# Power tables in another element order, longer Toeplitz loads and a wider margin in the written order, in an attention and state-space kernel

## Chip, cores and metric

The kernel runs on one core of a Trainium2 chip. The metric is device time in microseconds: the median of the runs. One more execution is recorded by the hardware profiler; all lines of profile and trace below come from that one.

## What is computed

Two branches over the same 2,048 tokens of width 448, mixed by a gate:

```python
g = sigmoid((x * gate_w).sum(-1, keepdims=True))
a = A_ref(x, wq, wk, wv, wo)      # 16 query heads of 28, ONE key and value head, softmax over 2048 keys
b = B_ref(x, A, B, C, log_dt, Dskip)
return g * a + (1 - g) * b

# B_ref: a diagonal state-space layer as a causal convolution, per channel d (448 of them)
K[d, l] = real(sum_n C[d,n] * dB[d,n] * exp(dt[d] * A[d,n] * l))     # n = 256 complex modes, l = 0..2047
y[:, d] = causal_convolution(u[:, d], K[d]) + u[:, d] * Dskip[d]
```

Tensors are bfloat16. Most of the arithmetic is the 16 x 2,048 x 2,048 exponentials of the softmax, the kernel K of 448 channels from 256 modes each, and the convolution of each channel.

## The kernel before

**Attention.** ScalarE takes the exponentials. The work is cut into 1,024 score tiles of 128 keys x 512 queries: 16 groups (`i`, 4 heads and 512 queries each), 16 key tiles, 4 heads. Tiles go in sets of three and two by turns. TensorE writes a set's scores into PSUM (five banks, lines 1103 and 1112), ScalarE takes the exponential of the set in one instruction (L1134) into a ring of 15 buffers, and TensorE multiplies by the values (L1144). For each group there are also a query projection (L759), copies of masked queries by GpSimd's DMA queue, a normalisation (`norm`, L1004 to L1014, with a path through DRAM for the reciprocals) and, every fourth group, the output projection (`outp`, L986) and its gated addition to the result `O` (L995).

**State space.** The 448 channels go in 14 chunks of 32. For each chunk:

1. `masters` (in four blocks of chunks, L796 to L818) squares the complex pole again and again on VectorE, so that powers 1, 2, 4, ... up to 1,024 steps exist.
2. `tables` (L820 to L873) builds on VectorE tables of 32 consecutive powers by doubling: five levels, each with two products (L850, L852), a difference (L854) and a sum (L856). A table row holds 128 values: 64 for the low powers (32 channels, two halves of the modes) and 64 for powers in steps of 32, seeded with the coefficients. The real table and the imaginary table are separate blocks of 33 rows (`BLK`). It also builds `rho` (L859, L863), a further table FM by a reversed product (L867), and negates the imaginary one (L872).
3. `kgen` (L875 to L912) makes K from these tables on TensorE, 128 matmuls of 64 columns per chunk (L889), each for one channel, one half of the modes, and the real or imaginary part. As neighbouring powers lie one row apart, its operands step 128 elements, 256 bytes. VectorE copies the result (L899, L902), and GpSimd's DMA queue writes it to a DRAM scratch tensor KP in nine stores. KP has for each channel a row of 1,088 elements, in two halves.
4. `conv` (L937 to L978), twice per chunk. `tload` (L924 to L935) loads for 4 channels the Toeplitz matrix: partition 2i + h reads the KP row of half h from element i on, 1,024 elements for each of 4 channels. It is two transfers, one per h, of 64 partitions x 4 rows of 2,048 bytes. There are 4 such loads per `conv`, 112 in all; they go to 4 buffers in T and later to up to 3 in the part of U (the input) that is no longer needed. Then 128 matmuls (L949), a gated copy to `cst` (L958), 16 transposing matmuls (L969), and an addition to `O` (L977).

**The order.** Nothing is ordered by hand. Every operation is recorded with an estimated duration, a rank (`pr`, low first), what it reads and writes, and if it needs one of two spare PSUM banks, a lock on one (`lock`, `unlock`). `schedule` (L156 to L276) then plays the whole program through with its own constants and fixes the order of each engine; at run time the engines only follow it and wait on semaphores. The constants that matter here: `SLACK` (L86) is time added to a dependency across engines for operations of rank 2 and up, by engine; `FETCH` (L82) is how long a new block of 256 TensorE instructions is taken to need; L138 and L140 price a DMA by its descriptors. GpSimd's queue carries the KP stores, the masked queries and the normalisation's small transfers; SP's queue carries the Toeplitz loads in order, each waiting for KP of its chunk and for the last reader of its buffer, and the stores of the result behind all of them.

Of the kernel before, what the change touches and what calls it, by code (L numbers as in the profile page):

```python
# [12 lines left out]
P = 128  # L13
# [12 lines left out]
LO = 2 * BLK  # L26
FM = 2 * LO
# [7 lines left out]
TW = 4 * 1024  # L35
# [39 lines left out]
class Prog:  # L75
# [6 lines left out]
    BLOCK, FIRST, FETCH, IDLE, NEED = 256, 172, 5300.0, 3300.0, 0.015  # L82
# [3 lines left out]
    SLACK = {"pe": 500.0, "dve": 300.0}  # L86
# [44 lines left out]
    def dma(self, pairs, desc, slot, rd=(), wr=(), pr=0, eng="sp", slow=False, extra=0):  # L131
# [6 lines left out]
        o = self.op(eng, fn, nd * ns / 16.0 * (1.15 if size < 1500 else 1.8 if nd < 512 else 1.0), rd, wr, pr)  # L138
# [237 lines left out]
class Kernel:  # L376
# [25 lines left out]
    def alloc(self):  # L402
# [26 lines left out]
        self.T = sb("T", NTR * TW + 768, BF)  # L429
# [212 lines left out]
    def xq(self, q):  # L642
        return ((self.xT, 0), (self.T, NTR * TW + 768 - XQ), (self.expT, 9 * 512), (self.expT, 5 * 512))[q]

# [26 lines left out]
    def prep_params(self):  # L671
# [71 lines left out]
        for s in range(2):  # L743
            o = s * LO + 32 * EW
            for comp, val in ((0, 1.0), (1, 0.0)):
                pg.op("dve", lambda e, o=o, comp=comp, val=val: e.memset(self.tab.v(0, P, o + comp * BLK, [[1, 64]]), val), 70,
                      wr=[("lo", s, 0)] + xd, pr=3)
# [72 lines left out]
    def tables(self, c):  # L820
# [6 lines left out]
        mq = lambda lv: self.mq.v(0, P, lv * W2 + 64 * c, [[1, 64]])  # L827
        pr = 50 + 2 * c

        def vo(fn, n, rd, wr, rate=1.92):  # L830
            pg.op("dve", fn, el(n, rate), rd=rd, wr=wr, pr=pr)
        mk = lambda lv: [("mb", lv), ("mb", lv + 6)]
        lk = lambda l: ("lo", s, l)
        vo(lambda e: e.tensor_copy(tab.v(0, P, lo + 31 * EW, [[BLK, 2], [1, 64]]), mbf.v(0, P, mo, [[128, 2], [1, 64]])),
           128, [("mb", 0), lk(0)], [lk(1)])
        vo(lambda e: e.tensor_copy(tab.v(0, P, lo + 31 * EW + 64, [[BLK, 2], [1, 64]]),
                                   self.seedw.v(0, P, c * 64, [[W2, 2], [1, 64]])),
           128, [("w32", b), ("w32b", b), lk(0)], [lk(2)])
        done = [lk(1), lk(2)]
        for lv in range(5):  # L840
# [3 lines left out]
            so, do = lo + (32 - w) * EW, lo + (32 - 2 * w) * EW  # L844
            src = tab.v(0, P, so, [[BLK, 2], [EW, w], [1, EW]])
            dst = tab.v(0, P, do, [[BLK, 2], [EW, w], [1, EW]])
            mr = mbf.v(0, P, m, [[0, 2], [0, w], [1, EW]])
            mi = mbf.v(0, P, m + 128, [[0, 2], [0, w], [1, EW]])
# [3 lines left out]
            vo(lambda e, src=src, mi=mi, w=w, tb=tb, to=to: e.tensor_tensor(  # L852
                tb.v(0, P, to, [[w * EW, 2], [EW, w], [1, EW]]), src, mi, ALU.mult), 2 * n, done + mk(lv), [tk])
            vo(lambda e, do=do, n=n, tb=tb, to=to: e.tensor_tensor(  # L854
                tab.v(0, P, do, [[1, n]]), tab.v(0, P, do, [[1, n]]), tb.v(0, P, to + n, [[1, n]]), ALU.subtract), n, [tk, kr], [kr])
            vo(lambda e, do=do, n=n, tb=tb, to=to: e.tensor_tensor(  # L856
                tab.v(0, P, do + BLK, [[1, n]]), tab.v(0, P, do + BLK, [[1, n]]), tb.v(0, P, to, [[1, n]]), ALU.add), n, [tk, ki], [ki])
            done = done + [kr, ki]
        vo(lambda e: e.tensor_copy(rho.v(0, P, 31 * 64, [[1, 64]]), mq(0)), 64,  # L859
           [("mq", 0)], ["tmp"])  # L860
        for lv in range(5):
            w = 1 << lv
            vo(lambda e, w=w, lv=lv: e.tensor_tensor(rho.v(0, P, (32 - 2 * w) * 64, [[64, w], [1, 64]]),  # L863
                                                     rho.v(0, P, (32 - w) * 64, [[64, w], [1, 64]]),
                                                     self.mq.v(0, P, lv * W2 + 64 * c, [[0, w], [1, 64]]), ALU.mult), w * 64,
               [("mq", lv), "tmp"], ["tmp"])
        vo(lambda e: e.tensor_tensor(tab.v(0, P, FM, [[64, 2], [EW, 32], [1, 64]]),  # L867
                                     tab.v(0, P, lo + 31 * EW, [[BLK, 2], [-EW, 32], [1, 64]]),
                                     rho.v(0, P, 31 * 64, [[0, 2], [-64, 32], [1, 64]]), ALU.mult), 4096,
           done + ["tmp"], ["Fm"])  # L870
        ni = tab.v(0, P, lo + BLK + EW, [[EW, 31], [1, 64]])
# [3 lines left out]
    def kgen(self, c):  # L875
# [6 lines left out]
        for jj in range(8):  # L882
            def mm(e, comp, jj=jj):
                for half in range(2):
                    for g in range(4):
                        o = half * 32 + 8 * g + jj
                        fo = lo + comp * BLK + EW + o
                        mo = FM + comp * 64 + o
                        r = e.matmul(  # L889
                            G.v(32 * g, 32, 64 * jj, [[1, 64]]),  # L890
                            tab.v(0, P, lo + comp * BLK + 64 + o, [[EW, 32]]),
                            tab.v(0, P, fo, [[mo - fo, 2], [EW, 32]]),
# [3 lines left out]
            for comp in range(2):  # L896
                pg.op("pe", lambda e, mm=mm, comp=comp: mm(e, comp), 226, mode="c", ni=16, rd=keys,
                      wr=[X, "kst", "kst2"], pr=1.4, lock=G if jj == 0 and comp == 0 else None)
# [15 lines left out]
    def tbufs(self):  # L914
        n = NC * 8
        home = [(self.T, k * TW, 0) for k in range(NTR)] + [(self.U, k * TW, (k + 1) * 32) for k in range(3)]
# [7 lines left out]
    def tload(self, gi):  # L924
# [6 lines left out]
        lst = []  # L931
        for h in range(2):
            to = bass.AP(tensor=buf.h, offset=h * buf.rs + o, ap=[[2 * buf.rs, 64], [1024, 4], [1, 1024]])
            lst.append((to, dram(self.KP, h * KH + 4 * gi * KW, [[1, 64], [KW, 4], [1, 1024]])))
        self.lastT = pg.dma(lst, (512, 2048), f"T{s}", rd=[("KP", gi // 8), "pad"] + x, wr=w, pr=1, extra=1500).i  # L935

    def conv(self, c):  # L937
# [3 lines left out]
        ps, px = self.grp(), self.grp()  # L941
# [287 lines left out]
```

## Time and profile before

| | us |
|---|---|
| three runs | 541.32, 544.85, 545.44 |
| median | 544.85 |
| the profiled execution | 546.33 |
| its span, first to last instruction | 544.5 |
| ScalarE: exponentials (L1134), 410 instructions | 468.1 busy |
| first exponential starts, last one starts | 30.5, 522.6 |
| TensorE busy, VectorE busy | 451.6, 455.3 |
| kernel matmuls L889: 1,792 | 69.0 busy |
| DMA: bytes moved | 144.55 MB, 265 GB/s in the mean |

The profile page gives for each engine its busy time; several instructions of TensorE overlap, so its busy time is not work at full rate. A group of instructions is written as line, engine, operation, names and shapes, count, then busy time and mean duration of one in ns, and after the second bar the idle time of the engine just before them and what ended it. A wait is written as who waited, for whom, then total us, how often, and the longest. A timeline row gives start and duration in us, and in brackets the idle time before it and what released it. "issue" means that the profile shows nothing that the engine waited for.

### The profile page before, as it was taken

The page shows a single profiled execution, that of the slowest core. Times are in us where ns is not written, and L with a number is a line of the kernel's source. Part 1 is how long each engine was busy: PE and PEld are TensorE (multiplying, and loading weights), DVE is VectorE, ACT ScalarE, POOL GpSimd, SP SyncE. Part 2 cuts the span into 40 slices and gives each one's busy share as a digit, 9 for nine tenths or more (in the row PEclk, how much of TensorE's full clock was granted, in tenths as well). Part 3 has the DMA queues.
Part 4 walks back from the last instruction along what each step waited for, and adds up shares of the span by engine and source line. Part 5 has one row for each costly group of instructions (what it writes and reads, how often), then busy time and mean ns, then how long its engine had stood idle before and what let it go on. Part 6 is the DMA issues. An engine that isn't in the chain of part 4 may idle for free.

```text
span 544.5 us, 20905 instructions
## 1 busy us (share of the span) xinstructions
PE 451.6 (83%) x9463; PEld 226.4 (42%) x9479; DVE 455.3 (84%) x826; ACT 485.9 (89%) x431; POOL 168.1 (31%) x313
## 2 busy tenths in 40 slices
PE   4787679688798989789788898889898898996875
PEld 3522114154353535345344445345454444352443
DVE  2889999999999989889989998989899999912024
ACT  3699899999999989899999999999999998997840
POOL 5017022515142413315215241515225060532100
PEclk9958888999999999899999999999899999998888
DMA  8995691696977697896994998798994999679996
GB/s 254 238 232 151 47 159 30 172 355 206 360 238 247 189 368 244 257 365 216 361 373 136 362 308 305 208 390 273 326 371 144 345 337 353 182 258 321 361 385 194
DMA packets 122401, 144.55 MB, mean 265 GB/s; under 512 B 54196, under 2 KB 60956, under 8 KB 122312
## 3 DMA queue, kind: packets, MB, share of 16 engines
q1 hardware_dynamic: 112312, 133.06, 75.9%
q0 software_dynamic: 9344, 9.59, 7.3%
q8 instruction: 74, 1.21, 0.9%
q10 hardware_dynamic: 656, 0.57, 0.4%
q14 instruction: 15, 0.12, 0.1%
HBM read 128.76 MB, written 5.28 MB: 246 GB/s over the span
## 4 chain that ended last, share of the span: by engine, by line
ACT 30%; PE 27%; DVE 19%; DMA 15%; issue 3%; SPq 0%
ACT expT L1134 30%; DMA T<-KP_scratch 9%; PE psS L1112 6%; DMA U<-KP_scratch 6%; PE psX L889 5%; PE psS L1103 4%; PE psB L1144 4%; PE psS L949 2%; PE psX L949 2%; DVE msq L796 2%; DVE tab L850 2%; DVE mbf L816 2%; DVE seedz L800 1%; PE psS L889 1%; DVE tmp L852 1%
## 5 line engine op out<-in xcount | busy, mean ns | idle before, releaser
L1134 ACT ACTIVATE expT<-psS 128x1536 bf16<-128x1536 f32 (+1 forms) x410 | 468.1, 1317 | 23.1 <-PE psS L1112 11.7
L1112 PE MATMUL psS<-qM,kT 128*32 128x512 bf16 x1660 | 134.3, 400 | 14.0 <-ACT expT L1134 10.6
L1103 PE MATMUL psS<-qT,kT 29*128 29x512 bf16 x609 | 82.9, 400 | 33.4 <-ACT expT L1134 29.6
L1144 PE MATMUL psB<-expT,vaug 128*32 128x512 bf16 x1024 | 104.7, 398 | 0.7 <-issue 0.4
L135 POOL DMA_DIRECT2D KP_scratch<-kstg x126 | 67.8, 546 | 70.7 <-DVE kstg L902 69.2
L850 DVE TENSOR_TENSOR tab<-tab,mbf 128x256 bf16<-128x256 bf16 (+4 forms) x70 | 68.6, 979 | 0.7
L1103 PEld LDWEIGHTS psS<-qT,kT 29*128 29x128 bf16 x609 | 19.9, 91 | 83.3 <-ACT expT L1134 72.9
L135 POOL DMA_DIRECT2D rdenB<-R_scratch x60 | 30.6, 517 | 75.8 <-DMA R_scratch<-denT 56.3
L889 PE MATMUL psX<-tab 128*32 128x64 bf16 x1280 | 49.5, 286 | 0.3 <-issue 0.2
L1112 PEld LDWEIGHTS psS<-qM,kT 128*32 128x32 bf16 x1660 | 30.4, 98 | 45.6 <-ACT expT L1134 34.7
L1144 PEld LDWEIGHTS psB<-expT,vaug 128*32 128x32 bf16 x1024 | 27.4, 96 | 49.9 <-issue 38.2
L135 POOL DMA_DIRECT2D qM<-qT x64 | 32.1, 509 | 43.4 <-DVE gt L638 20.4
L889 PEld LDWEIGHTS psX<-tab 128*32 128x32 bf16 x1280 | 39.4, 135 | 11.3 <-issue 3.9
L949 PE MATMUL psX<-T,U 128*32 128x128 bf16 (+7 forms) x1568 | 34.4, 221 | 9.0 <-DMA T<-KP_scratch 5.9
L135 POOL DMA_DIRECT2D denT<-acc x15 | 11.3, 756 | 97.5 <-DVE acc L1004 97.5
L949 PE MATMUL psS<-T,U 128*32 128x128 bf16 (+7 forms) x1216 | 30.2, 222 | 9.5 <-DMA T<-KP_scratch 6.7
L852 DVE TENSOR_TENSOR tmp<-tab,mbf 128x256 bf16<-128x256 bf16 (+3 forms) x56 | 36.3, 648 | 0.0
L949 PEld LDWEIGHTS psX<-T,U 128*32 128x32 bf16 (+7 forms) x1568 | 26.5, 94 | 20.3 <-DMA T<-KP_scratch 8.1
L867 DVE TENSOR_TENSOR tab<-tab,tmp 128x4096 bf16<-128x4096 bf16 x14 | 32.1, 2290 | 0.4
L852 DVE TENSOR_TENSOR tab<-tab,mbf 128x4096 bf16<-128x4096 bf16 x14 | 31.9, 2278 | 0.0
L949 PEld LDWEIGHTS psS<-T,U 128*32 128x32 bf16 (+7 forms) x1216 | 21.7, 95 | 21.0 <-DMA T<-KP_scratch 6.9
L863 DVE TENSOR_TENSOR tmp<-tmp,mq 128x64 bf16<-128x64 bf16 (+4 forms) x70 | 25.3, 361 | 1.2
(153 smaller groups left out, 553.4 us busy)
## 6 DMA issues: line engine op xcount, KB each, us to landing
T<-KP_scratch SPq DMA_DIRECT2D x174, 512.0 KB, 9.3
U<-KP_scratch SPq DMA_DIRECT2D x50, 512.0 KB, 9.5
rdenB<-R_scratch POOLq DMA_DIRECT2D x60, 64.0 KB
U<-cst SPq DMA_DIRECT2D x1, 3584.0 KB, 19.0
qM<-qT POOLq DMA_DIRECT2D x64, 32.0 KB, 5.2
tab<-in_A_x_dram SPq DMA_DIRECT2D x4, 448.0 KB, 6.2
O<-in_A_x_dram SPq DMA_DIRECT2D x16, 112.0 KB, 2.7
O<-cst SPq DMA_DIRECT2D x1, 1792.0 KB, 27.1
```

The source lines that it names most:

```text
L135: return [e.dma_start(o, i, **kw) for o, i in pairs]
L796: pg.op("dve", lambda e: e.tensor_tensor(m2(msq), z2, z2, ALU.mult), el(2 * n), rd=[kr, ki] + first, wr=["msq"], pr=pr)
L850: vo(lambda e, dst=dst, src=src, mr=mr: e.tensor_tensor(dst, src, mr, ALU.mult), 2 * n, done + mk(lv), [kr, ki])
L852: vo(lambda e, src=src, mi=mi, w=w, tb=tb, to=to: e.tensor_tensor(tb.v(0, P, to, [[w * EW, 2], [EW, w], [1, EW]]), src, mi, ALU.mult), 2 * ...
L863: vo(lambda e, w=w, lv=lv: e.tensor_tensor(rho.v(0, P, (32 - 2 * w) * 64, [[64, w], [1, 64]]), rho.v(0, P, (32 - w) * 64, [[64, w], [1, 64]]),
L867: vo(lambda e: e.tensor_tensor(tab.v(0, P, FM, [[64, 2], [EW, 32], [1, 64]]), tab.v(0, P, lo + 31 * EW, [[BLK, 2], [-EW, 32], [1, 64]]), r ...
L889: r = e.matmul(G.v(32 * g, 32, 64 * jj, [[1, 64]]), tab.v(0, P, lo + comp * BLK + 64 + o, [[EW, 32]]), tab.v(0, P, fo, [[mo - fo, 2], [EW, ...
L949: r = e.matmul(ps.v(32 * j, 32 - 2 * n, 128 * k, [[1, 128]]), self.U.v(0, P, (4 * gi + j) * 32 + 2 * n, [[1, 32 - 2 * n]]), tbuf.v(0, P, t ...
L1103: r = e.matmul(self.psS.v(0, P, 512 * b, [[1, 512]]), kT.v(32 * h, DH + 1, 128 * kt, [[1, 128]]), qT.v(32 * h, DH + 1, 512 * (i % 2), [[1, ...
L1112: r = e.matmul(self.psS.v(32 * j, 32, 512 * b, [[1, 512]]), kT.v(0, P, 128 * kt + 32 * j, [[1, 32]]), self.qM.v(0, P, (i % 2) * XQ + 512 * ...
L1134: pg.op("act", lambda e: e.activation(expT.v(0, P, 512 * es[0], spread(es, n)), self.psS.v(0, P, 512 * bs[0], spread(bs, n)), AF.Exp, scal ...
L1144: r = e.matmul(self.psB.v(32 * h, 32, 0, [[1, 512]]), vaug.v(0, P, 32 * kt, [[1, 32]]), expT.v(0, P, 512 * ring[t], [[1, 512]]), start=(kt ...
```

## The change

- **Tables.** A chunk's tables are laid out with a pair of channels innermost, then real and imaginary part, then the step: four values (8 bytes) per step, 33 steps per pair (`CG` = 132 elements), 64 pairs. Products (L850, L852) cover whole runs; the difference, the sum, the reversed product and the negation touch every other pair of values. The reversed product becomes two instructions. `kgen`'s operands now step 4 elements, 8 bytes; the scheduler's price for eight of its matmuls goes from 226 to 130 ns.
- **Loads.** One transfer of 128 partitions per Toeplitz load, each partition one row of 3 x 1,088 + 1,024 = 4,288 elements, 8,576 bytes, that runs over the unused ends of the rows between. Buffers grow from 4,096 to 4,288 elements, and the three in U come into use 8 loads later.
- **Scheduler.** `SLACK` of VectorE from 300 to 800 ns, `FETCH` from 5,300 to 5,600; a convolution's result and its transposes share one spare PSUM bank; the output projection's rank goes from 2 to 1.2.

```diff
-    BLOCK, FIRST, FETCH, IDLE, NEED = 256, 172, 5300.0, 3300.0, 0.015
+    BLOCK, FIRST, FETCH, IDLE, NEED = 256, 172, 5600.0, 3300.0, 0.015
-    SLACK = {"pe": 500.0, "dve": 300.0}
+    SLACK = {"pe": 500.0, "dve": 800.0}
-TW = 4 * 1024
+TW = 3 * KW + 1024
...
 # tables
-            src = tab.v(0, P, so, [[BLK, 2], [EW, w], [1, EW]])
-            dst = tab.v(0, P, do, [[BLK, 2], [EW, w], [1, EW]])
-            mr = mbf.v(0, P, m, [[0, 2], [0, w], [1, EW]])
+            src = tab.v(0, P, so, [[CG, 64], [2, 2 * w], [1, 2]])
+            dst = tab.v(0, P, do, [[CG, 64], [2, 2 * w], [1, 2]])
+            dc = [tab.v(0, P, do + 2 * k, [[CG, 64], [4, w], [1, 2]]) for k in range(2)]
+            mr = mbf.v(0, P, m, [[2, 64], [0, 2 * w], [1, 2]])
...
-            vo(lambda e, do=do, n=n, tb=tb, to=to: e.tensor_tensor(
-                tab.v(0, P, do, [[1, n]]), tab.v(0, P, do, [[1, n]]), tb.v(0, P, to + n, [[1, n]]), ALU.subtract), n, [tk, kr], [kr])
+            vo(lambda e, dc=dc, tc=tc: e.tensor_tensor(dc[0], dc[0], tc[1], ALU.subtract), n, [tk, kr], [kr])
+            vo(lambda e, dc=dc, tc=tc: e.tensor_tensor(dc[1], dc[1], tc[0], ALU.add), n, [tk, ki], [ki])
...
-        vo(lambda e: e.tensor_tensor(tab.v(0, P, FM, [[64, 2], [EW, 32], [1, 64]]),
-                                     tab.v(0, P, lo + 31 * EW, [[BLK, 2], [-EW, 32], [1, 64]]),
-                                     rho.v(0, P, 31 * 64, [[0, 2], [-64, 32], [1, 64]]), ALU.mult), 4096,
-           done + ["tmp"], ["Fm"])
-        ni = tab.v(0, P, lo + BLK + EW, [[EW, 31], [1, 64]])
+        for k in range(2):
+            vo(lambda e, k=k: e.tensor_tensor(tab.v(0, P, FM + 2 * k, [[EW, 32], [4, 32], [1, 2]]),
+                                              tab.v(0, P, lo + 124 + 2 * k, [[CG, 32], [-4, 32], [1, 2]]),
+                                              rho.v(0, P, 62, [[64, 32], [-2, 32], [1, 2]]), ALU.mult), 2048,
+               done + ["tmp"], ["Fm"])
+        ni = tab.v(0, P, lo + 6, [[CG, 32], [4, 31], [1, 2]])
 # kgen
-                            tab.v(0, P, lo + comp * BLK + 64 + o, [[EW, 32]]),
-                            tab.v(0, P, fo, [[mo - fo, 2], [EW, 32]]),
+                            tab.v(0, P, so, [[4, 32]]),
+                            tab.v(0, P, fo, [[mo - fo, 2], [4, 32]]),
...
-                pg.op("pe", lambda e, mm=mm, comp=comp: mm(e, comp), 226, mode="c", ni=16, rd=keys,
+                pg.op("pe", lambda e, mm=mm, comp=comp: mm(e, comp), 130, mode="c", ni=16, rd=keys,
 # tload
-        for h in range(2):
-            to = bass.AP(tensor=buf.h, offset=h * buf.rs + o, ap=[[2 * buf.rs, 64], [1024, 4], [1, 1024]])
-            lst.append((to, dram(self.KP, h * KH + 4 * gi * KW, [[1, 64], [KW, 4], [1, 1024]])))
-        self.lastT = pg.dma(lst, (512, 2048), f"T{s}", rd=[("KP", gi // 8), "pad"] + x, wr=w, pr=1, extra=1500).i
+        self.lastT = pg.dma([(buf.v(0, P, o, [[1, TW]]), dram(self.KP, 4 * gi * KW, [[1, 64], [KH, 2], [1, TW]]))], (128, 2 * TW), f"T{s}", rd=[("KP", gi // 8), "pad"] + x, wr=w, pr=1, extra=1500).i
 # conv
-        ps, px = self.grp(), self.grp()
+        ps = px = self.grp()
...
-                                     tbuf.v(0, P, to + j * 1024 + 896 - 128 * n, [[1, 128]]),
+                                     tbuf.v(0, P, to + j * KW + 896 - 128 * n, [[1, 128]]),
...
-              el(512), rd=[X, "omq"], wr=[("cst", cs)], pr=2, unlock=ps)
+              el(512), rd=[X, "omq"], wr=[("cst", cs), X], pr=2)
```

## Prediction

> **What bounds the kernel now.** I read the busy shares first, then ScalarE's waits, then what TensorE did just before each of those waits, then the last 30 us, then VectorE's groups by shape.
>
> ```profile
> PE 451.6 (83%) x9463; PEld 226.4 (42%) x9479; DVE 455.3 (84%) x826; ACT 485.9 (89%) x431; POOL 168.1 (31%) x313
> ```
>
> ScalarE is the fullest, and the others are close behind. From its first exponential (30.5 us) to the end of its last (523.2) lie 492.7 us, of which the exponentials fill 468.1. The waits say where the rest is:
>
> ```profile
> ACT expT L1134 <- PE psS L1112: 11.7, 13, 2.4
> ACT expT L1134 <- PE psS L1103: 8.3, 12, 1.5
> ACT expT L1134 <- PE psX L949: 1.3, 1, 1.3
> ACT expT L1134 <- PE psB L1144: 0.9, 1, 0.9
> ```
>
> That is 22.2 us in 27 waits, all for scores that TensorE delivered late. TensorE's timeline ahead of each shows two causes:
>
> ```profile
> 411.81 0.40 PE L949 MATMUL psS<-T,U 128*24 128x128 bf16 x16 [1.02 <-issue]
> ...
> 500.00 0.94 PE L949 MATMUL psX<-T,U 128*32 128x128 bf16 x28 [2.01 <-DMA T<-KP_scratch]
> ```
>
> Line two is a convolution that waited 2.01 us for its Toeplitz load; the exponential behind it came 2.37 us late. Line one is "issue": TensorE waited for nothing the profile names. Going through the 24 breaks in ScalarE's timeline after 85 us, 10.9 us stand behind a load and 5.8 us behind an "issue" gap. The remaining 5.5 us are small or lie before 85 us. None stands behind a wait for the power tables.
>
> The end of the span, by windows (us, TensorE, weight loads, VectorE, ScalarE, GpSimd, granted clock, DMA share, GB/s):
>
> ```profile
> 523.00:525.00 2.00, 1.54 (x57) 1.24 (x53) 0.78 (x2) 0.24 (x1) 0.00 (x0) 1.00 1.05 386
> 533.00:535.00 2.00, 2.00 (x23) 0.86 (x25) 0.47 (x1) 0.00 (x0) 0.00 (x0) 0.72 1.08 341
> 535.00:537.00 2.00, 1.23 (x63) 0.87 (x52) 1.96 (x4) 0.00 (x0) 0.00 (x0) 1.00 0.83 245
> 537.00:539.00 2.00, 1.78 (x75) 1.19 (x77) 1.02 (x3) 0.00 (x0) 0.00 (x0) 1.00 0.19 53
> ```
>
> The DMA engines are full until 536.5, 13.3 us after the last exponential; 8 us more carry the last convolution, its fold and the store. So the time is: start 30.5, exponentials and the waits in them 492.7, tail 21.3.
>
> VectorE is nearly as tight: in the nine 40-us windows from 85 to 445 us it is busy 340.2 of 360, so 19.8 are free. Its shapes:
>
> ```profile
> L867 DVE TENSOR_TENSOR tab<-tab,tmp 128x4096 bf16<-128x4096 bf16 x14 | 32.1, 2290 | 0.4
> L796 DVE TENSOR_TENSOR msq<-seedz 128x512 f32<-128x512 f32 x30 | 20.4, 682 | 0.1
> L854 DVE TENSOR_TENSOR tab<-tab 128x2048 bf16<-128x2048 bf16 x14 | 17.0, 1212 | 0.0
> L872 DVE TENSOR_SCALAR tab<-tab 128x1984 bf16<-128x1984 bf16 x14 | 9.7, 693 | 0.3
> L800 DVE TENSOR_TENSOR seedz<-msq 128x256 f32<-128x256 f32 x30 | 12.4, 414 | 0.0
> L977 DVE TENSOR_TENSOR O<-O,psS 128x256 bf16<-128x256 bf16 x15 | 6.2, 413 | 7.7 <-PE psS L969 7.6
> ```
>
> **The change, part by part.**
>
> *Kernel matmuls (kgen).* 1,792 matmuls of 64 columns read tables with a step of 256 bytes. The chain shows them as pieces of 32 in 0.89 us, 28 ns each, 50 us of TensorE. Afterwards the step is 8 bytes. Cheap end: a convolution's matmuls with contiguous operands follow each other 32 in 0.45 us (507.31 to 507.76), 14 ns, and half their columns would make 7. Dear end: the transposes L969, which also step, do 16 in 0.45 us, 28 ns, as now. I take 14, as the step comes close to contiguous: 25 us of TensorE saved (0 to 37). L889 holds 5.7% of the chain that ended last, 31 us, so half of it looks like a gain of 15. It isn't: no late exponential was late for these matmuls alone, and scores can't run ahead of ScalarE by more than the five banks. I book 2 us, for catching up after a gap faster (0 to 5).
>
> *Table instructions on VectorE.* The number of elements stays. One multiplication per chunk (L867, 2290 ns) becomes two of 2048 (1212 each): 134 ns by 14 chunks, 1.9 us. The four memsets are well under 1 us. What is new is the pattern: products still run over at least 8 adjacent bytes, but sums and differences (L854, L856), the reversed product (L867) and the negation (L872) take 4 bytes and skip 4. No row of the trace does that in SBUF. One end: nothing; L977 hops 64 bytes per element in PSUM and takes 413 ns, as the contiguous L800 does (414). The other end: these instructions fall to half rate. The slope is 0.52 ns per element in bf16 (2290 against 1212) and 1.05 in f32 (682 against 414 for 256 fewer). Sums, differences and reversed products are 12,032 elements per chunk, 6.3 us more; the negation 0.5 us more; by 14, 95 us. A gain is excluded, since no instruction gets fewer elements. I take nothing, as the hopping row is the nearer one, and keep 95 for the range. The 1.9 us are covered by the 19.8 us that VectorE has free.
>
> [...]
>
> *Toeplitz loads.* 224 transfers of 524 KB in rows of 2,048 bytes become 112 of 128 rows of 8,576 bytes, 1.098 MB: 4.7% more bytes than the pair they replace. In the full windows from 515 to 527 us DMA moves 377 GB/s, so 2.78 us becomes 2.91 per load, 15 us in all. That is spread over windows whose DMA share is 0.59 to 0.96; only where loads queue does it count. No row has such long rows, so the rate has to be bounded. Better end: the page's best slice, 390 GB/s, 2.81 us. Worse end: the poorest full window, 341, 3.22 us. I take 377. An issue costs SP 0.62 us (two in 1.24), and there is one instead of two, so a load with nothing ahead is complete up to 0.6 us sooner. That is worth half of a typical late load (the listed ones are 0.2 to 2.4).
>
> *Order.* Counted in score tiles (1,024 in all, 0.48 us each) by the order of TensorE's instructions, chunk 13's kernel matmuls end at tile 955 before and at 985 after; the earlier chunks also move back by 10 to 40 tiles. So each convolution is placed later against its tables, and VectorE gets 30 tiles, 14 us, more for its last tables. Their nine stores on GpSimd's queue move with them. Chunk 0 shows the way from kgen to loads: matmuls over at 92.5, SP's first load at 99.9, 7.4 us. After: 39 tiles before the last exponential is -18.7 us, loads of chunk 13 may start at -11.3. Loads 102 and 103 wait for buffers freed at tiles 995 and 1000, so they stand ahead until about -8. Then 8 loads of 2.91 us end at +15.3, against +13.3 now. Tail: 2 us longer (2.81 us each: +1; 3.22 each: +4).
>
> *Waits.* Of the 10.9 us behind loads I take half away, for the one issue and the later places (0 to all); of the 5.8 us at "issue" gaps, 1.5, since the kernel's scheduler now allows 5.6 us for a block of instructions in place of 5.3 (0 to 4). A convolution and its transposes now share one PSUM group: the transposes already waited for the read of that group (L958), so no wait is added; what queues behind the longer hold is the next kgen, query projection or convolution. This and the output projection's rank are in the order that I counted; I price them at nothing (a wait for a group would show as at most the 0.7 us of an L958).
>
> **Sum**, against the profiled execution (546.33, its span 544.5 and 1.8 around it; it stands 1.5 above the median 544.85): kgen -2, waits behind loads -5.4, issue -1.5, tail +2, VectorE 0: -6.9, so 539.4, and 538 against the median.
>
> **Rivals.**
> - *VectorE falls behind.* Sums, reversed products and negation at half rate, 95 us. For it: no such row, and a VectorE 94% full. Against: the hopping row. The order hides 14 us and the free time up to 19.8, so it decides from 14 to 34 us on; the full price gives 544.85 + 95 + 2 - 34 to 544.85 + 95 + 2 - 14, 608 to 628: slower. Chance 0.15.
> - *The tail eats it.* The waits stay, since they are set by when slots come free, and the later chunk 13 makes the tail 1 to 4 us longer, or up to 10 if the loads ahead of chunk 13 slip by two (5.8 us). With kgen's -2 and with nothing from kgen that is 544 to 555. For it: the DMA engines are full in the tail. Chance 0.25.
> - *All load and issue waits go*, 16.7 us, and the kgen gain is 5: 544.85 - 21.7 + 2 = 525, if the tail still costs 2. For it: 25 us of TensorE free. Chance 0.12.
> - *The matmuls don't get faster at all*: my 2 us are lost, 540. It lies inside the likeliest case.
>
> **How the numbers follow.** Likeliest, chance 0.48: 538, own range 530 to 545. The others as above. Leaving out the case of 608 and more and the far ends takes 0.17 to 0.2: range 522 to 558. A measurement can tell about 1%, so faster means under 539.4, slower over 550.3. Faster: 0.12 and some 0.38 of the likeliest case, 0.50. Slower: 0.15 and 0.09 of the second rival, 0.24. The rest, 0.26, is the same.
>
> **What would show it.** L889 in pieces of 32 in about 0.45 us. L854's 128x2048 form at about 1212 ns: at 2,200 the first rival has won. The waits of the exponential near 15 us, with fewer TensorE rows released by T or U. Last exponential near 516, DMA full until 15 us after it. I am wrong if a table instruction releases kgen, if the loads run far from 2.9 us, or if new waits come from the longer hold of a PSUM group.

## The result and the profile after

The changed kernel takes 559.38 us (median of four runs, 557.77 to 561.6), beside 545.08 for the kernel before on the same chip: ratio 1.0281, 95% interval 1.022 to 1.0342. It is slower. The forecast was 538, its range ended at 558, and the likeliest of the rivals that end slower was "the tail eats it", 544 to 555.

The profiled execution took 560.53 us, its span 558.7, 14.2 more than the span before. The first exponential starts at 28.2 us (30.5 before), the last ends at 528.9 (523.2), and the tail after it is 29.8 us (21.3). So 2.3 us are won at the start, 8.0 lost between the exponentials and 8.5 behind them.

The busy times of the engines, from the page after:

```profile
PE 446.8 (80%) x9463; PEld 208.8 (37%) x9479; DVE 461.4 (83%) x840; ACT 486.0 (87%) x431; POOL 167.5 (30%) x313
```

ScalarE does the same work. VectorE has 6.1 us more, TensorE 4.8 less busy time. The waits of the exponentials (total us, times, longest):

```profile
ACT expT L1133 <- PE psS L1102: 14.9, 21, 2.2
ACT expT L1133 <- PE psS L1111: 14.2, 13, 2.6
```

That is 29.1 us where 22.2 were. I went through both traces with one rule: each wait of an exponential is put down to the longest gap of TensorE just ahead of it. Loads stand for 10.1 us before and 4.7 after, "issue" gaps for 6.7 and 13.2, everything else for 4.5 and 10.0; about a microsecond of each total lies in waits before 40 us, which the rule leaves out. (Read by eye, the forecast had 10.9 and 5.8 for the first two of before.) The three longest gaps after are all "issue", here two of them in TensorE's timeline:

```profile
504.47 0.61 PE L1111 MATMUL psS<-qM,kT 128*32 128x512 bf16 x7 [2.66 <-issue]
...
524.00 0.19 PE L968 MATMUL psX<-ident,cst 128*64 128x64 bf16 x1 [2.49 <-issue]
```

Before, the longest "issue" gap was 1.58. TensorE's granted clock differs too. Here it is from 85 to 500 us (length of the window, then the columns as before) before, after, and in g4, a run described below:

```profile
85.00:500.00 415.00, 359.75 (x8133) 182.03 (x8139) 374.52 (x668) 399.53 (x351) 140.44 (x261) 0.99 0.84 279
85.00:500.00 415.00, 348.81 (x7992) 161.46 (x8009) 383.39 (x687) 393.70 (x346) 135.14 (x251) 0.96 0.77 282
85.00:500.00 415.00, 358.31 (x8142) 166.07 (x8143) 377.96 (x679) 397.96 (x349) 140.72 (x260) 0.96 0.82 288
```

g4 has the same 0.96 and takes as long as the kernel before, so a clock of 0.96 doesn't make the loss by itself; how much of "everything else" is due to it is not shown.

The end of the span, first by windows:

```profile
525.00:530.00 5.00, 4.15 (x107) 2.30 (x99) 0.00 (x0) 3.86 (x4) 0.00 (x0) 0.66 1.01 418
530.00:535.00 5.00, 4.25 (x33) 3.05 (x34) 3.07 (x6) 0.00 (x0) 0.00 (x0) 1.00 0.95 384
535.00:540.00 5.00, 1.84 (x56) 1.07 (x60) 3.30 (x6) 0.00 (x0) 0.00 (x0) 0.93 1.01 420
540.00:545.00 5.00, 3.46 (x128) 3.19 (x132) 0.00 (x0) 0.00 (x0) 0.00 (x0) 0.50 0.42 158
```

The long rows move 418 to 420 GB/s in full windows (377 before). But from 540 to 545 the DMA engines are not full, although a load is still to come. SP's queue shows why:

```profile
520.97 0.51 SPq L136 DMA_DIRECT2D U<-KP_scratch  x1
527.69 0.51 SPq L136 DMA_DIRECT2D T<-KP_scratch  x1
529.34 1.16 SPq L136 DMA_DIRECT2D U<-KP_scratch  x2
530.54 0.71 SPq L136 DMA_DIRECT2D T<-KP_scratch  x1
543.61 0.51 SPq L136 DMA_DIRECT2D U<-KP_scratch  x1
```

The last load is issued at 543.61, 13 us after the one ahead of it. The chain that ended last tells what released it:

```profile
529.89 12.58 DMA U<-KP_scratch
542.48 0.04 issue
542.52 1.09 PE psX L948 x33
543.61 6.77 DMA U<-KP_scratch
550.38 0.04 issue
550.43 1.07 PE psS L948 x32
```

Load 104 goes to the third buffer in U. It is the first load there, and that buffer now covers columns of U that convolution 25, loads 100 to 103, has to read first (the last of its matmuls run from 529.11 to 529.72). So it is issued only at 529.89, as the second of the pair at 529.34, lands at 542.5, and load 111, which has the same buffer, can only follow. Before, that buffer came into use at load 96, and the last load was issued at 524.38 us, with the DMA engines full until 536.5.

VectorE's groups by shape: the split reversed product, the difference at two sizes, and in the last line the smaller difference before (busy us, mean ns):

```profile
L869 DVE TENSOR_TENSOR tab<-tab,tmp 128x2048 bf16<-128x2048 bf16 x28 | 34.3, 1224 | 0.6
L857 DVE TENSOR_TENSOR tab<-tab 128x2048 bf16<-128x2048 bf16 x14 | 17.1, 1224 | 0.0
L857 DVE TENSOR_TENSOR tab<-tab,tmp 128x512 bf16<-128x512 bf16 x14 | 6.3, 453 | 0.2
...
L854 DVE TENSOR_TENSOR tab<-tab,tmp 128x512 bf16<-128x512 bf16 x14 | 5.8, 415 | 0.2
```

The large ones keep their rate (1212 before); the differences of 512 elements and fewer take 38 to 60 ns more.

### The profile page after: what moved, and what is told of

Read it like the earlier page. It is cut to its first block, busy times and chain, and to the rows that moved or that the text cites. A ratio compares the mean times of both kernels' runs of the same rounds, so it can differ in the third digit from the quotient of the medians.

```text
span 558.7 us, 20811 instructions
## 1 busy us (share of the span) xinstructions
PE 446.8 (80%) x9463; PEld 208.8 (37%) x9479; DVE 461.4 (83%) x840; ACT 486.0 (87%) x431; POOL 167.5 (30%) x313
## 4 chain that ended last, share of the span: by engine, by line
ACT 46%; PE 25%; DMA 12%; DVE 11%; issue 5%; ACTq 0%
ACT expT L1133 46%; DMA T<-KP_scratch 7%; PE psS L1111 6%; PE psS L1102 4%; PE psB L1143 4%; DMA U<-KP_scratch 3%; PE psS L760 2%; PE psX L892 2%; PE psS L948 2%; PE psX L948 1%; DVE tab L869 1%; DVE tab L857 1%; DMA seedw<-in_gate_w_dram 1%; DVE tab L852 1%; PE psS L892 1%
## 5 line engine op out<-in xcount | busy, mean ns | idle before, releaser
L1133 ACT ACTIVATE expT<-psS 128x1536 bf16<-128x1536 f32 (+1 forms) x410 | 468.3, 1317 | 29.9 <-PE psS L1102 14.9
L1111 PE MATMUL psS<-qM,kT 128*32 128x512 bf16 x1660 | 139.4, 408 | 23.3 <-ACT expT L1133 13.7
L1102 PE MATMUL psS<-qT,kT 29*128 29x512 bf16 x609 | 86.4, 411 | 41.3 <-ACT expT L1133 37.4
L1143 PE MATMUL psB<-expT,vaug 128*32 128x512 bf16 x1024 | 109.2, 412 | 6.2 <-issue 6.2
L852 DVE TENSOR_TENSOR tab<-tab,mbf 128x256 bf16<-128x256 bf16 (+4 forms) x70 | 68.4, 980 | 0.7
L1102 PEld LDWEIGHTS psS<-qT,kT 29*128 29x128 bf16 x609 | 20.4, 92 | 97.3 <-ACT expT L1133 79.2
L1111 PEld LDWEIGHTS psS<-qM,kT 128*32 128x32 bf16 x1660 | 29.2, 98 | 63.6 <-ACT expT L1133 43.2
L948 PE MATMUL psX<-T,U 128*32 128x128 bf16 (+7 forms) x1408 | 37.3, 231 | 6.5 <-DMA T<-KP_scratch 4.6
L948 PE MATMUL psS<-T,U 128*32 128x128 bf16 (+3 forms) x1472 | 34.4, 223 | 2.4 <-DMA T<-KP_scratch 1.9
L869 DVE TENSOR_TENSOR tab<-tab,tmp 128x2048 bf16<-128x2048 bf16 x28 | 34.3, 1224 | 0.6
L948 PEld LDWEIGHTS psX<-T,U 128*32 128x32 bf16 (+7 forms) x1408 | 26.5, 99 | 19.9 <-issue 7.0
L948 PEld LDWEIGHTS psS<-T,U 128*32 128x32 bf16 (+3 forms) x1472 | 26.0, 95 | 14.5 <-DMA T<-KP_scratch 3.8
L136 POOL DMA_DIRECT2D R_scratch<-denT x15 | 8.6, 573 | 62.9 <-DVE denT L1009 37.6
L797 DVE TENSOR_TENSOR msq<-seedz 128x512 f32<-128x512 f32 (+1 forms) x40 | 25.4, 634 | 0.1
## 6 DMA issues: line engine op xcount, KB each, us to landing
U<-KP_scratch SPq DMA_DIRECT2D x22, 1072.0 KB, 10.9
```

Of the source, the lines that this page charges most:

```text
L136: return [e.dma_start(o, i, **kw) for o, i in pairs]
L797: pg.op("dve", lambda e: e.tensor_tensor(m2(msq), z2, z2, ALU.mult), el(2 * n), rd=[kr, ki] + first, wr=["msq"], pr=pr)
L852: vo(lambda e, dst=dst, src=src, mr=mr: e.tensor_tensor(dst, src, mr, ALU.mult), 2 * n, done + mk(lv), [kr, ki])
L869: vo(lambda e, k=k: e.tensor_tensor(tab.v(0, P, FM + 2 * k, [[EW, 32], [4, 32], [1, 2]]), tab.v(0, P, lo + 124 + 2 * k, [[CG, 32], [-4, 32 ...
L948: r = e.matmul(ps.v(32 * j, 32 - 2 * n, 128 * k, [[1, 128]]), self.U.v(0, P, (4 * gi + j) * 32 + 2 * n, [[1, 32 - 2 * n]]), tbuf.v(0, P, t ...
L1102: r = e.matmul(self.psS.v(0, P, 512 * b, [[1, 512]]), kT.v(32 * h, DH + 1, 128 * kt, [[1, 128]]), qT.v(32 * h, DH + 1, 512 * (i % 2), [[1, ...
```

## The experiments

Eighteen kernels ran. The labels of the theories in the expectations: 1, long rows delay TensorE's instruction fetches; 2a, the later order makes the tail; 2b and 5, the later buffers in U make it; 3, TensorE is held by the fetch of instruction blocks, so shorter matmuls buy nothing; 4, the order alone is the cause. "Waits" are those of the exponentials from the first one on, "gaps" TensorE's "issue" gaps of 0.15 us or more and "loads" its waits on transfers, both from 85 us to the last exponential (in the expectations 11.6 is the gaps of before with those behind it, 10.5 without). These four and the tail come from the one profiled execution of each run. A ratio is to the kernel before as it ran beside that run (medians of 543.0 to 545.7 us).

| run | us | ratio, 95% | waits | tail | gaps | loads |
|---|---|---|---|---|---|---|
| before | 545.1 | 1 | 22.2 | 21.3 | 10.5 | 15.2 |
| after | 559.4 | 1.0281 (1.022 to 1.0342) | 29.1 | 29.8 | 21.4 | 6.4 |
| a1 short rows | 561.1 | 1.0265 (1.0197 to 1.0333) | 30.4 | 29.8 | 20.9 | 7.2 |
| a7 third buffer from 107 | 552.5 | 1.011 (1.0074 to 1.0146) | 26.0 | 24.5 | 23.8 | 4.8 |
| a2 old constants | 561.5 | 1.0271 (1.0196 to 1.0347) | 32.4 | 25.1 | 19.9 | 9.2 |
| a3 tables alone | 547.6 | 1.0029 (0.9988 to 1.0071) | 27.4 | 18.7 | 14.2 | 7.8 |
| a4 long rows alone | 560.9 | 1.0271 (1.0214 to 1.0328) | 43.4 | 17.6 | 14.1 | 20.4 |
| a6 constants alone | 578.4 | 1.0596 (1.0521 to 1.067) | 27.0 | 49.3 | 9.2 | 6.9 |
| a8 shared group alone | 545.9 | 1.004 (0.9996 to 1.0084) | 28.3 | 18.5 | 12.1 | 13.0 |
| a9 change without loads | 564.5 | 1.0352 (1.0278 to 1.0426) | 20.3 | 40.1 | 8.6 | 11.8 |
| f1 all work, old order | 555.7 | 1.0234 (1.0189 to 1.0279) | 33.0 | 21.3 | 6.6 | 26.3 |
| f2 old work, new order | 578.3 | 1.0635 (1.0585 to 1.0686) | 47.4 | 28.3 | 9.9 | 23.2 |
| f3 tables, old order | 545.4 | 1.0019 (0.999 to 1.0048) | 24.3 | 20.5 | 13.0 | 12.5 |
| f4 long rows, old order | 556.3 | 1.0221 (1.0184 to 1.0257) | 32.8 | 21.7 | 4.9 | 22.5 |
| g1 late buffers, short rows | 556.4 | 1.0224 (1.0184 to 1.0263) | 35.5 | 18.3 | 5.7 | 27.5 |
| g2 long rows, old buffers | 545.8 | 1.0002 (0.9979 to 1.0025) | 22.5 | 21.6 | 7.1 | 16.2 |
| g4 tables, long rows, old buffers | 545.5 | 1.0012 (0.9981 to 1.0044) | 24.7 | 20.3 | 7.9 | 16.2 |
| g5 half the kernel matmuls | 537.4 | 0.9851 (0.9817 to 0.9885) | 22.4 | 19.9 | 1.9 | 18.2 |
| h1 early buffers, old constants | 551.6 | 1.0163 (1.0119 to 1.0207) | 24.8 | 20.0 | 15.5 | 8.6 |
| h2 early buffers, new constants | 566.5 | 1.0398 (1.0333 to 1.0464) | 22.5 | 44.1 | 14.1 | 9.8 |

### Rows and third buffer in the changed kernel (a1, a7)

a1 splits each load again and keeps every engine's order:

```diff
-        self.lastT = pg.dma([(buf.v(0, P, o, [[1, TW]]), dram(self.KP, 4 * gi * KW, [[1, 64], [KH, 2], [1, TW]]))], (128, 2 * TW), f"T{s}", rd=[("KP", gi // 8), "pad"] + x, wr=w, pr=1, extra=1500).i
+        lst = []
+        for h in range(2):
+            to = bass.AP(tensor=buf.h, offset=h * buf.rs + o, ap=[[2 * buf.rs, 64], [KW, 4], [1, 1024]])
+            lst.append((to, dram(self.KP, h * KH + 4 * gi * KW, [[1, 64], [KW, 4], [1, 1024]])))
+        self.lastT = pg.dma(lst, (128, 2 * TW), f"T{s}", rd=[("KP", gi // 8), "pad"] + x, wr=w, pr=1, extra=1500).i
```

(The scheduler counts the two issues as one, so that the order stays.)

> The changed kernel with every instruction in the same order on every engine, but each Toeplitz load again as two transfers with rows of 2,048 bytes, into the same buffers. Theory 1 (the longer 'issue' gaps of TensorE, 21.4 us against 11.6, come from instruction fetches that stand behind rows of 8,576 bytes): the gaps after 85 us fall back to 11 to 14 us with none over 1.7, the waits of the exponentials (29.1) fall to 19 to 22, and the time to 549 to 553, though the tail may grow by 1 to 2 with the slower loads. Rival (the gaps come from the order or from the faster kernel matmuls): gaps of 19 to 23 us, waits of 28 or more, 558 to 562.

561.1 us, gaps 20.9, tail 29.8, all as in the changed kernel: theory 1 falls. The rows neither lengthen the gaps (21.4 with them) nor buy anything (559.4).

a7 changes one number of the buffers' first loads:

```diff
-(self.U, k * TW, 8 + (k + 1) * 32)
+(self.U, k * TW, (40, 72, 107)[k])
```

> The changed kernel with the third buffer in U first given to load 107 in place of load 104; the order of the matmuls of the exponentials' stage is the same. Theory 2b (the tail is longer because load 104 is the first in the third buffer, waits until convolution 25 has read its columns of U, and load 111 then waits for the convolution of 104): the tail after the last exponential falls from 29.8 us to 19 to 23, and the time to 549 to 553. Rival 2a (the tail is longer only because chunk 13's kernel matmuls come later in the order): tail of 28 to 30, 557 to 561.

552.5 us, in 2b's range; the tail fell by 5.3 us to 24.5, not quite to the 19 to 23. SP's last loads are now issued earlier:

```profile
525.88 1.16 SPq L136 DMA_DIRECT2D U<-KP_scratch  x2
527.09 6.81 SPq L136 DMA_DIRECT2D T<-KP_scratch  x2
533.94 12.76 SPq L136 DMA_DIRECT2D out_dram<-O  x8
```

The last load is now issued by 533.9 and goes into T. So about half of the loss is this one buffer.

### Each part alone, with an order worked out anew (a2, a3, a4, a6, a8, a9)

a2 sets the three constants back in the changed kernel; a6 below makes the opposite edit in the kernel before.

```diff
-    BLOCK, FIRST, FETCH, IDLE, NEED = 256, 172, 5600.0, 3300.0, 0.015
+    BLOCK, FIRST, FETCH, IDLE, NEED = 256, 172, 5300.0, 3300.0, 0.015
-    SLACK = {"pe": 500.0, "dve": 800.0}
+    SLACK = {"pe": 500.0, "dve": 300.0}
-                rd=["Wo"] + [("on", gg) for gg in range(4)], wr=[X], pr=1.2, lock=G if g == 0 else None)
+                rd=["Wo"] + [("on", gg) for gg in range(4)], wr=[X], pr=2, lock=G if g == 0 else None)
```

> The changed kernel with the three constants of the order as before (fetch 5,300 ns, VectorE's slack 300 ns, the output projection's rank 2). Counted in score tiles, chunk 13's kernel matmuls end at 970 in place of 985. Rival 2a (order alone makes the tail): the tail falls by 7 us to 22 or 23, time 550 to 553. Theory 2b (third buffer): load 104 still waits for convolution 25, so the tail falls by 3 us at most, 555 to 559 in all. For the gaps: theory 1 keeps them at 19 to 23 us; if the constants make them they fall to 11 to 14.

561.5 us: no gain, and above both ranges. The tail fell by 4.7, and the waits rose by 3.3. The gaps stay at 19.9, so it is not the constants that make them.

a3 takes `tables`, `kgen`, the memsets and `CG` of the change, as the diff of the change has them, into the kernel before.

> The kernel before with the new power tables and the kernel matmuls that read them, and nothing else of the change. Theory 1: gaps of 10 to 13 us as before, waits of the exponentials 19 to 23, chunk 13's kernel matmuls 5 tiles later, tail 21 to 24: 541 to 547. Rival (the faster kernel matmuls or slower tables make the gaps and waits): gaps of 17 or more, waits of 27 or more, 549 to 555.

547.6 us, 0.6 over the range; the interval of its ratio holds 1. The waits are 27.4, so the rival has them right, but the tail gives 2.6 back.

a4 takes `tload`, `tbufs`, the larger buffers (`TW`) and the scheduler's price for such a load from the change, alone; a9 is the opposite, the changed kernel with those of before. a8 takes the shared group alone:

```diff
-        ps, px = self.grp(), self.grp()
+        ps = px = self.grp()
-              el(512), rd=[X, "omq"], wr=[("cst", cs)], pr=2, unlock=ps)
+              el(512), rd=[X, "omq"], wr=[("cst", cs), X], pr=2)
```

> The kernel before with the 8,576-byte loads alone (their buffers, so the third one in U from load 104 on, and their entry in the order's costs). Counted in score tiles the order then puts chunk 13's kernel matmuls at 923 in place of 955, and load 111's convolution before the last exponential. Theory (the place of chunk 13 and of the third buffer in the order sets the tail; long rows cost nothing by themselves): the tail falls from 21.3 us to 12 to 17, the gaps stay at 10 to 14, 535 to 543. Rival (long rows or their buffers cost time by themselves): tail of 20 or more or waits of the exponentials of 29 or more, 548 to 556.

560.9 us: the rival. The tail did fall to 17.6, but one exponential waited 19.05 us at 393.9, behind three convolutions in a row that waited for loads (5.9 us in all; the rest is other work that the order put ahead of the next scores):

```profile
386.44 1.04 PE L945 MATMUL psS<-T,U 128*32 128x128 bf16 x32 [2.01 <-DMA T<-KP_scratch]
389.69 1.04 PE L945 MATMUL psS<-U 128*32 128x128 bf16 x32 [2.20 <-DMA U<-KP_scratch]
392.42 1.04 PE L945 MATMUL psS<-T,U 128*32 128x128 bf16 x32 [1.69 <-DMA T<-KP_scratch]
```

> The kernel before with the three constants of the order alone (fetch 5,600 ns, VectorE's slack 800 ns, the output projection's rank 1.2). Chunk 13's kernel matmuls stand at tile 991 in place of 955, and the last 16 convolutions behind the last scores. Theory (the later order lengthens the tail): 36 tiles are 17 us, of which the waits for loads inside the stage (some 10 us) are the other side: tail 30 to 38, 551 to 562. Rival (the constants buy as much inside the stage as they cost behind it): 543 to 548.

578.4 us, far above the range: the tail is 49.3. The constants put the convolutions of the last sixteen loads behind all scores.

> The kernel before with the convolution and its transposes in one PSUM group, and nothing else of the change. Chunk 13 stands at tile 965 in place of 955. Theory (the group costs only what the order makes of it, 10 tiles): tail 21 to 26, 544 to 549. Rival (the longer hold of the group delays kernel matmuls, projections and convolutions): waits of the exponentials of 28 or more, 550 to 556.

545.9 us: free, though its waits (28.3) are the rival's, and a tail of 18.5, shorter than the theory's, pays for them.

> The changed kernel with the loads of before (two transfers of 2,048-byte rows, buffers of 4,096 columns, so the third one in U from load 96 on); tables, shared group and constants as changed. Chunk 13's kernel matmuls stand at tile 990 (985 in the changed kernel). Theory (the third buffer's later start made 5 to 7 us of the tail): tail 22 to 26, 550 to 555. Rival (the loads' layout has no part in it): tail 28 to 32, 557 to 563.

564.5 us: a miss for theory and rival. The waits fall to 20.3, the best of all kernels with the full computation, and the tail rises to 40.1. As in a6, the convolutions of the last sixteen loads stand behind all scores. So an order worked out anew is a confounder: each edit also moves the convolutions between stage and tail.

### The order held fixed (f1 to f4)

These replace the scheduler's choice by a recorded order of every engine; only SP takes loads as their buffers come free.

```diff
-                    key = (r, o.pr, i)
-                    if best is None or key < best[0]:
+                i = next((i for i in (queue[e] if e == "sp" else queue[e][:1]) if i in ready[e]), None)
```

> All the new work (tables, kernel matmuls, 8,576-byte loads, third buffer in U from load 107) with two PSUM groups per convolution as before, put into the order that the kernel before had on every engine (only SP takes the loads as their buffers come free). Theory 4 (the order, not the work, made the changed kernel slower): 538 to 547. Rival (the new work itself costs time, by later buffers or by instruction fetches that the faster kernel matmuls run into): 550 to 557.

> The work of before (tables, kernel matmuls, 2,048-byte loads, third buffer from load 96) with the shared PSUM group, put into the order that the changed kernel had on every engine. Theory 4: as slow as the changed kernel but for the wait for the third buffer (some 7 us), 550 to 558. Rival: 543 to 548.

> The kernel before with the new tables and kernel matmuls, in exactly the order of before on every engine. Theory 3 (a block of 256 TensorE instructions takes 5.6 us or more to be fetched, so faster kernel matmuls mostly turn into waits at the ends of blocks): 541 to 546, gaps 2 to 6 us longer than 10.5. Rival (the time of the kernel matmuls counts): 530 to 539.

> The kernel before with the 8,576-byte loads alone, the third buffer in U from load 107 in place of 96, in the order of before on every engine (only SP takes the loads as their buffers come free). Theory 4 (in a good order the rows cost nothing): 541 to 547. Rival (six buffers in place of seven from load 96 to 106 make the loads late): 549 to 558, with more than 20 us of TensorE's waits on loads.

f1 took 555.7 us: theory 4 falls, the work costs time in the old order too. f2 took 578.3, but can't be read as the order's price: TensorE waits 5.25, 8.47 and 5.87 us for exactly the loads 32, 64 and 96, the first in each U buffer, since its order was made for buffers that open at 40, 72 and 104. f3 is as fast as before: the tables with their faster matmuls are worth nothing, as theory 3 had it (gaps 13.0 for 10.5). f4 has the whole loss, 556.3, with 22.5 us of waits on loads, two of them long:

```profile
504.79 0.94 PE L1008 MATMUL psX<-U 128*32 128x128 bf16 x28 [4.38 <-DMA U<-KP_scratch]
...
521.29 1.04 PE L1008 MATMUL psX<-U 128*32 128x128 bf16 x32 [5.59 <-DMA U<-KP_scratch]
```

They are the 97th and the 103rd in TensorE's order; as two convolutions interleave there, the buffers and PSUM banks that they use make them loads 100 and 102. f1 has the same two waits, of 4.17 and 5.33 us. Long rows or late buffers, f4 can't tell.

### Rows or buffers, length or number (g1, g2, g4, g5)

All four keep the order of before. g1 is the kernel before with later buffers and nothing else; g2 has long rows in T's four buffers and the old form in U; g4 adds the tables to g2; g5 is f3 without half of its kernel matmuls. The edits of g1, g2 (in `tload`) and g5:

```diff
-(self.U, k * TW, (k + 1) * 32)
+(self.U, k * TW, (40, 72, 107)[k])

+        if s < NTR:
+            self.lastT = pg.dma([(buf.v(0, P, o, [[1, TW]]), dram(self.KP, 4 * gi * KW, [[1, 64], [KH, 2], [1, TW]]))],
+                                (128, 2 * TW), f"T{s}", rd=[("KP", gi // 8), "pad"] + x, wr=w, pr=1, extra=1500).i
+            return

-                for half in range(2):
+                for half in (comp,):
                     for g in range(4):
```

> The kernel before with nothing changed but the loads from which the three buffers in U are used: 40, 72 and 107 in place of 32, 64 and 96; order as before on every engine (only SP takes the loads as their buffers come free). Theory 5 (the later buffers cost the time, not the rows): as the long rows with these buffers, 552 to 560, with waits of 4 us or more on loads into U near 505 and 521 us. Rival (the rows of 8,576 bytes): 543 to 548.

556.4 us, and the same two waits, at the same loads:

```profile
508.84 0.94 PE L1012 MATMUL psX<-U 128*32 128x128 bf16 x28 [4.84 <-DMA U<-KP_scratch]
...
525.16 1.04 PE L1012 MATMUL psX<-U 128*32 128x128 bf16 x32 [5.04 <-DMA U<-KP_scratch]
```

> The kernel before with the 8,576-byte loads in the four buffers of T alone, and the three buffers in U as before (2,048-byte rows, from loads 32, 64 and 96); order as before. Theory 5: 540 to 547. Rival (the rows): half and more of the 12 us, 550 to 557.

545.8 us. With g1 this settles it: in one and the same order the late buffers cost 11 us, the long rows in T's buffers nothing.

> The new tables and kernel matmuls with the 8,576-byte loads in the four buffers of T, the buffers in U and the order as before. If both halves of the change cost nothing by themselves and the rows save a little, 539 to 545, not above the kernel before; a time of 548 or more would mean that they disturb each other.

545.5 us: the new tables, their matmuls and the long rows in T are free together, and gain nothing.

> The tables in the order of before, with half of the kernel matmuls left out (four of eight in each group: 896 of 1,792, so half of the products that make the Toeplitz rows are missing). Theory 3 (what the end of a block waits for is the fetch, so it is the number of instructions that counts and not their length): gaps of 10.5 to 13 us fall to 5 to 9, time 534 to 541. Rival (neither counts, since the exponentials set the pace): 542 to 546.

537.4 us, 0.9851, and gaps of 1.9 us. The change takes 16 us off TensorE by shorter matmuls, and nothing is gained (f3). Leaving out 896 of them at 19 ns, 17 us, gains 8. In the profiled executions, of which g5's is its slowest, the difference to f3 is 4.3. There the gaps fall by 11.1 us, but the waits of the exponentials by 1.9 only, since TensorE's waits for loads rise from 12.5 to 18.2. And g5's 17 us come on top of f3's 16. So that the number of instructions decides, and not the time that they take, is likely but not shown.

### Buffers and constants in the changed kernel (h1, h2)

Both get g2's edit of the loads; h1 also a2's of the constants.

> The changed kernel (tables, 8,576-byte rows in the four buffers of T, shared PSUM group) with the buffers in U as before and the three constants of the order as before; the order is worked out anew (chunk 13's kernel matmuls at tile 970). Theory 5 (with both taken back, the rest of the change is free): 542 to 549. Rival (the pieces disturb each other): 553 to 562.

> The changed kernel with the buffers in U as before, the new constants kept (chunk 13's kernel matmuls at tile 995, 16 convolutions behind the last scores). From the constants alone (tail 49 us) and the change without the loads (tail 40 us): tail 35 to 45, 557 to 568. Rival (the constants suit the new tables and rows, only the late buffers were wrong): 540 to 549.

551.6 us for h1, between the two expectations, and 566.5 for h2, with a tail of 44.1. With after (late buffers, new constants: 1.0281) and a2 (late, old: 1.0271) the four pairs are complete: only early buffers with the old constants gain, and then 1.0163 remains. h1 does the work of g4 apart from the shared group, in another order, and g4 is at 1.0012. That rest lies in the order worked out anew, or in the shared group, which was free in a8; what exactly costs it stays open. Its gaps are 15.5 us, g4's 7.9.

No kernel with the full computation came out faster than the one before.

## Why the forecast was wrong

In the profiled executions the sum gave 539.4 us, and 560.5 came, 21.1 more. The tail holds 6.5 of them (2 more forecast, 8.5 more came). The stage of the exponentials holds 16.9 (8.9 less forecast, 8.0 more came): 8.0 behind "issue" gaps, 5.5 in waits put down to neither a load nor such a gap, 2 of the kernel matmuls, and 1.4 in smaller pieces. The earlier start took 2.3 off.

- **The step that failed in the tail is "Order", its last part:** "Then 8 loads of 2.91 us end at +15.3". I let the eight loads follow each other. I had the places of loads 102 and 103, but priced the later opening of the U buffers at nothing and did not look at who is first in the third one. The loads did start in time. The first of chunk 13 (load 105) is issued 11.0 us before the last exponential ends, where I had 11.3:

```profile
517.87 0.51 SPq L136 DMA_DIRECT2D T<-KP_scratch  x1
```

But the last one landed 21.5 us after that end, not 15.3. One number for the third buffer gave 5.3 us of the tail and 7 of the time back (a7). In the old order buffers that open at 40, 72 and 107 cost 11 us (g1). So it is not the later opening alone, since a7 opens the third buffer later still, for load 107 in place of 104; it matters which load is the first in it.

- **The step that failed in the stage is in "Waits":** "This and the output projection's rank are in the order that I counted; I price them at nothing". I had counted the places of chunk 13, not what a new order does to the scores. The waits put down to neither a load nor an "issue" gap rose from 4.5 to 10.0 us, and those at the gaps too (below). The shared group alone has 28.3 us of waits (a8) and the constants alone 27.0 (a6), for 22.2 before; in the old order the new tables and long rows have 24.7 (g4). Early buffers in place of late ones lower the waits by 7.6 us with the old constants (a2 to h1) and by 6.6 with the new ones (after to h2, which loses more in the tail). So part of it goes with the new order and part with the late buffers; as each of these orders is worked out anew, the shares stay open.
- **Waits behind loads, -5.4:** 10.1 to 4.7 is -5.4. Right in size, and partly by luck: the one issue has little part in it (TensorE's waits on loads are 7.2 us in a1 with two, 6.4 after), and these waits were traded for the tail, as a2, a9 and h2 show: whoever defers convolutions waits less for their loads and has more of them left at the end.
- **Waits at "issue" gaps, -1.5:** they rose by 6.5. What I took for a better allowance in the scheduler hardly shows: the constants alone have gaps of 9.2 for 10.5 (a6), and the old ones put back 19.9 for 21.4 (a2). Before and after, 74 packets of 16,384 bytes come on the instruction queue for 18,942 matmuls and weight loads (67 for 17,166 in g5), some 256 to a packet. Counting TensorE's instructions, all 12 gaps of 0.6 us or more after, and all eight before, fall at the same place of a run of 256 (instruction 177 to 187, slowly drifting), and each ends 1.3 to 1.6 us after such a packet has landed. From the entry into one block to the landing of the next one's packet pass some 4.1 us in the median, before and after, and at most some 6.3. In these 20 places TensorE was through with a block before the landing and those 1.3 to 1.6 us were over. Blocks that ended right on their packet (within 1.7 us) are some 22 before, 30 after, 29 in f3 and at most 12 in g5; the edge of a block is known to a few instructions only. Of the 74 packets after, 12 have a gap of 0.6 us or more behind them, so most blocks begin without one; yet "issue" gaps stand behind 13.2 of the 29.1 us of waits.
- **Kernel matmuls, 14 ns and 2 us:** they take 19 ns (56 in 1.07 us), between my cheap and dear ends, so 16 us of TensorE were saved for 25 expected. Worth on the clock: nothing (f3), where I booked 2. The lines, a piece of the chain before and TensorE's timeline after:

```profile
285.87 0.89 PE psX L889 x32
...
499.62 1.07 PE L892 MATMUL psX<-tab 128*32 128x64 bf16 x56
```

- **Tables, 0:** right. No half rate (1224 ns for 1212 at 2,048 elements); VectorE has 6.1 us more, of which 2.2 are the split product (34.3 for 32.1); most of the rest is at the small sizes. The first rival is out.
- **Loads, 2.91 us:** 1.098 MB at 418 GB/s is 2.63. Mis-sized to the good side, and worth nothing (a1, g2).
- **Start, not in the sum:** the first exponential came 2.3 us earlier. a6 has it at 28.0 and a8 at 27.6, h1 at 30.6, and g1 and g2, in the order of before, at 29.9 and 29.4; what moves it is open.
- **The rivals:** "the tail eats it" had the right place for 8.5 of the 14.2 us and the wrong cause: chunk 13's loads started when forecast, and a buffer held up the last of them. With 10 us at most it was too small, since the waits in the stage came on top.

## What to carry to other kernels

When a buffer grows, list which transfer is first in each buffer and what must have read that memory: three buffers that opened 8, 8 and 11 loads later cost 11 us here, more than any of the instructions that were argued about. On an engine that streams small instructions, making them shorter can buy nothing (19 ns for 28 after, a ratio of 1.0019 in f3), and leaving some out may (0.9851 in g5, though it takes out time as well as number); look for gaps that recur at one place of a run of instructions, as all 20 of 0.6 us or more did here, before and after, in runs of 256. Where a planner makes the order, hold its order fixed before giving a part its price, for each edit also shifts work between stage and tail.

## What was unexpected

- A block of 256 TensorE instructions takes 6.2 us in the median after, and the next block's packet lands some 4.1 us after its start; as the gaps ended 1.3 to 1.6 us after a landing, less than a microsecond is left in the median. Rows of 8,576 bytes in the data queue did not delay that packet (the medians after and in a1, with 2,048, lie within 0.25 us of each other).
- Rows of 8,576 bytes moved 418 to 420 GB/s in full windows, those of 2,048 some 377 to 388 (338 and 341 in the two poorest windows of 2 us).
- A step of 8 bytes in TensorE's two operands gave 19 ns per 64-column matmul, one of 256 bytes 28.
- On VectorE differences over every second 4-byte word took as long as contiguous ones at 2,048 elements (1224 for 1212 ns), and 38 ns longer at 512 (453 for 415).
